# Pooled attention keys in pieces of 64, 16 and 64 turned by identity products, with a new instruction order and choice of engines

## The chip, the cores and the metric

The kernel runs on one core of one Trainium2 chip. The metric is the time of one execution on the device in microseconds (us), the median of several runs. Durations below come from one profiled execution. PE is TensorE, which multiplies; PEld is its loading of weights; DVE is VectorE, ACT ScalarE, POOL GpSimd, and SP SyncE, whose queue issues all transfers here.

## What is computed

Two parts in one kernel. First, attention over 8 batches, 8 heads, 576 positions, 64 values a head, as the sum of two attentions: one over positions pooled by four (144 of them, its output repeated four times), one in which a position sees only neighbours less than 4 away. Then an FFN on the 4608 rows that this gives, with 1024 hidden values and a SoLU with layer norm.

```python
q_d = q.reshape(B, H, Sd, factor, D).mean(axis=3)        # factor 4, Sd = 144; k_d, v_d alike
out_d = sm_attn(q_d, k_d, v_d)                           # softmax over the 144 pooled keys
out_up = np.repeat(out_d, factor, axis=2)
mask = np.abs(pos[:, None] - pos[None, :]) < factor
scores = np.where(mask, scale * np.matmul(q, k.transpose(0, 1, 3, 2)), -1e9)
out_local = softmax(scores) @ v
x = (out_up + out_local), heads side by side             # 4608 x 512
h = x @ w_in                                             # 512 x 1024
solu = h * softmax(h)
ln = (solu - mean) / np.sqrt(var + 1e-6) * g_ln
out = ln @ w_out                                         # 1024 x 512
```

The weights and g_ln are float64 as they arrive in memory. The other arrays are float32.

## The kernel before

**Attention.** A batch works on head pairs, since two heads of 64 fill 128 partitions. q and k are brought to partitions = head values (`qT`, `kT`): for the first two batches by products with the identity (`qp`, `kp`), later by the DVE's transpose of 32x32 blocks. `sums` adds each four positions (`qd`, `kd`).

`Pooled` is the pooled attention of one head pair; a batch has four. Its 144 queries are handled as 3 pieces of 48 (`QC`, `QN`). Its steps: `sd`, the scores, 6 products on 64x64 quadrants of the array; the maximum (`mxd`); the exponentials `pd` with their sums; `pd` times the reciprocal sums; `pdt`, the scores turned so that keys lie on partitions, 12 transposes of 64x72 in two halves of 72 keys; `pdT`, two copies from PSUM; `po`, 4 products of the turned scores with the pooled values `vd`, each over 72 keys; and the sum into `x`.

`Local` is the local attention of two windows of 64 positions for all heads; a batch has five. Its steps: `sc`, the scores, 16 products on quadrants; `pl`, the scores plus the mask; the maximum `mxl` and its subtraction; the exponentials; their sums `sml`, reciprocals `rsl` and the product with them; `plt`, four 128x128 transposes; `plT`, their copy; `xp`, 16 products on quadrants with the values `vw`; and the sum into `x`.

The pooled values `vd` are made of `vs`, four loads a batch of 72 pooled positions x 4 heads, each added up by two additions.

**Weights.** `Weights.piece` turns a 128x512 piece of float64 into float32 with four DVE operations and splits it into a high part and a rest (`wi_h`, `wi_l`; `wo_h`, `wo_l`), so that a product of float32 precision is three products of the faster type. There are 8 pieces of w_in and 8 of w_out; those of w_out are multiplied by g first.

**FFN.** 36 tiles of 128 rows. A tile: `xh`, `xl` are the split of `x`; `h`, 24 products of 128x512; the maximum `nmx`; the exponentials `e`; `e` times `h`; the centred values written to memory (`u`) and read back block by block (`v`); a 32x32 block transpose on DVE, the split `uh`, `ul`; `o`, 24 products with w_out; the scaled output `osb`.

**Order.** All steps of all parts are put in one list, `plan`. `ORDER` is a table of numbers that says in which order they are issued; each engine then runs its own instructions in that order and waits for what it needs. `keep_clock` issues 24 pairs of products of zeros (`warm`), which keep PE running in its idle time. Which engine runs a step is written in the step.

Of the kernel before, what the change touches and what calls it, by code (L numbers as in the profile page):

```python
# [129 lines left out]
def pooled_local_attention_then_solu_ffn(  # L130
# [31 lines left out]
    qhi = qlo[1:] + [S]  # L162

    QC = 3
    QN = SD // QC


    TILES = ((0, 0), (1, 1), (0, 1), (1, 0))
# [873 lines left out]
```

## Time and profile before

| what | value |
|---|---|
| median of 3 runs | 601.65 us (601.19 to 605.02) |
| the profiled execution, whole time | 602.74 us |
| its span in the profile | 601.0 us |
| mean granted clock of PE | 0.989 |
| busy: PE, DVE, ACT, POOL | 574.8, 396.5, 361.8, 375.6 us |
| bytes moved | 94.34 MB, 157 GB/s on average |

How to read the rows: a busy time is the sum of an engine's instructions. A product's duration reaches into the next one, since products are pipelined, so the time that a group takes is read from the starts. "A <- B" names what ended the idle time before A. A form such as 64*64 64x58 is the rows and columns of the array that a product uses, and the partitions x columns that it writes.

### The profile page before, as it was taken

How to read it: one execution, taken by the hardware profiler on the slowest of the kernel's cores; microseconds unless marked ns; L12 is line 12 of the kernel's file. 1: busy time of each engine (PE TensorE's matmuls, PEld its weight loads, DVE VectorE, ACT ScalarE, POOL GpSimd, SP SyncE). 2: the span in 40 equal slices, each digit the busy share in tenths (PEclk: the TensorE clock that was granted, in tenths of full speed). 3: DMA queues.
4: the chain of work that ended last, by engine and by line, in shares of the span. 5: the costliest groups of instructions: out<-in, count | busy, mean ns of one | idle time of the engine just before them, and what ended most of it. 6: DMA issues, size and time to landing. Idle time of an engine off the chain costs nothing.

```text
span 601.0 us, 15341 instructions
## 1 busy us (share of the span) xinstructions
PE 574.8 (96%) x5912; PEld 447.1 (74%) x5912; DVE 396.5 (66%) x692; ACT 361.8 (60%) x800; POOL 375.6 (62%) x553
## 2 busy tenths in 40 slices
PE   6889789899999999999999999999999999999996
PEld 3666557677777777787877777777777878788785
DVE  5989999869747677766856767737655533643541
ACT  3758866577745566566664854657465655553443
POOL 2576668867784778678574777656786767332221
PEclk8979999899999999999999999999999999999999
DMA  8999776687769767766878567847416623124230
GB/s 231 238 251 254 140 183 146 164 178 162 195 144 189 171 167 186 170 148 175 190 151 201 143 173 182 185 114 195 97 59 188 146 89 114 63 88 151 96 123 35
DMA packets 203913, 94.34 MB, mean 157 GB/s; under 512 B 162496, under 2 KB 192704, under 8 KB 203840
## 3 DMA queue, kind: packets, MB, share of 16 engines
q1 hardware_dynamic: 203840, 93.37, 63.3%
q8 instruction: 46, 0.75, 0.6%
q14 instruction: 27, 0.22, 0.1%
HBM read 65.54 MB, written 27.79 MB: 155 GB/s over the span
## 4 chain that ended last, share of the span: by engine, by line
PE 75%; POOL 6%; DVE 5%; ACT 4%; SPq 4%; DMA 3%; issue 3%; POOLq 0%; DVEq 0%
PE o L888 31%; PE h L770 27%; PE xp L670 3%; PE plt L660 3%; PE po L752 3%; PE sc L614 2%; DMA qm<-in_q_dram 2%; SPq L245 2%; PE pdt L731 2%; PE sd L696 2%; POOL pl L639 2%; DMA v<-u 1%; SPq L264 1%; POOL pd L720 1%; DVE w L334 1%
## 5 line engine op out<-in xcount | busy, mean ns | idle before, releaser
L888 PE MATMUL o<-wo_h,uh 128*128 128x512 f32 x288 | 117.9, 409 | 0.8 <-ACT uh L872 0.7
L770 PE MATMUL h<-wi_h,xh 128*128 128x512 f32 x288 | 116.3, 404 | 0.6 <-DVE e L785 0.6
L770 PE MATMUL h<-wi_h,xl 128*128 128x512 f32 x288 | 114.3, 397 | 1.3 <-POOL xl L922 1.3
L888 PE MATMUL o<-wo_l,uh 128*128 128x512 f32 x288 | 114.5, 398 | 0.0
L770 PE MATMUL h<-wi_l,xh 128*128 128x512 f32 x288 | 114.1, 396 | 0.0
L874 POOL TENSOR_TENSOR ul<-v,uh 128x512 fp32r<-128x512 f32 x58 | 74.4, 1288 | 19.7 <-ACT uh L872 7.7
L778 DVE TENSOR_REDUCE nmx<-h 128x1 f32<-128x1024 f32 x36 | 43.9, 1219 | 63.8 <-PE h L770 63.8
L888 PE MATMUL o<-wo_h,ul 128*128 128x512 f32 x288 | 79.1, 396 | 0.4 <-DVE ul L874 0.4
L782 ACT ACTIVATE e<-h,nmx 128x1024 f32<-128x1024 f32 x36 | 40.0, 1112 | 51.0 <-DVE nmx L778 51.0
L888 PEld LDWEIGHTS o<-wo_h,uh 128*128 128x128 f32 x288 | 54.6, 190 | 15.6 <-ACT uh L872 1.4
L770 PEld LDWEIGHTS h<-wi_h,xl 128*128 128x128 f32 x288 | 54.2, 188 | 15.2 <-POOL xl L922 2.1
L770 PEld LDWEIGHTS h<-wi_h,xh 128*128 128x128 f32 x288 | 54.2, 188 | 14.8 <-issue 1.0
L888 PEld LDWEIGHTS o<-wo_h,ul 128*128 128x128 f32 x288 | 54.2, 188 | 14.0 <-DVE ul L874 0.8
L770 PEld LDWEIGHTS h<-wi_l,xh 128*128 128x128 f32 x288 | 54.3, 189 | 12.2
L888 PEld LDWEIGHTS o<-wo_l,uh 128*128 128x128 f32 x288 | 54.5, 189 | 11.8
L922 POOL TENSOR_TENSOR xl<-x,xh 128x512 fp32r<-128x512 f32 (+1 forms) x40 | 47.1, 1183 | 18.6 <-ACT xh L919 17.4
L807 ACT ACTIVATE e<-e,nmu 128x1024 f32<-128x1024 f32 x35 | 40.1, 1146 | 28.2 <-POOL nmu L790 28.1
L785 DVE SCALAR_TENSOR_TENSOR e<-h,e 128x1024 f32<-128x1024 f32 x36 | 43.7, 1214 | 19.9 <-ACT e L782 19.9
L650 POOL TENSOR_TENSOR pl<-pl,rsl 128x512 f32<-128x512 f32 x40 | 42.1, 1055 | 20.7 <-DVE rsl L648 18.2
L866 DVE STREAM_TRANSPOSE v<-v 128x512 f32<-128x512 f32 x70 | 46.3, 688 | 12.5 <-DMA v<-u 12.5
L872 ACT ACTIVATE uh<-v 128x512 fp32r<-128x512 f32 x70 | 42.9, 623 | 14.9 <-DVE v L866 11.0
L639 POOL TENSOR_TENSOR pl<-pl,mxl 128x512 f32<-128x512 f32 x40 | 41.8, 1052 | 9.0 <-DVE mxl L637 4.6
(95 smaller groups left out, 1076.1 us busy)
## 6 DMA issues: line engine op xcount, KB each, us to landing
u<-e SPq DMA_DIRECT2D x35, 512.0 KB
v<-u SPq DMA_DIRECT2D x140, 128.0 KB
vw<-in_v_dram SPq DMA_DIRECT2D x160, 64.0 KB
vs<-in_v_dram SPq DMA_DIRECT2D x32, 288.0 KB
out_dram<-osb SPq DMA_DIRECT2D x36, 256.0 KB
qm<-in_q_dram SPq DMA_DIRECT2D x96, 72.0 KB
km<-in_k_dram SPq DMA_DIRECT2D x96, 72.0 KB
w<-in_moe_w_out_dram SPq DMA_DIRECT2D x8, 512.0 KB
```

What stands on the lines that cost most here:

```text
L639: nc.gpsimd.tensor_tensor(out=pl, in0=pl, in1=max_bc, op=ALU.subtract)
L650: nc.gpsimd.tensor_tensor(out=pl, in0=pl, in1=rs.unsqueeze(3).broadcast_to([P, NPR, 2, W]), op=ALU.mult)
L770: nc.tensor.matmul(hps[:, n, :], src[:, cc, :], wt[:, cc, n * 512:(n + 1) * 512], start=(cc == 0 and src is xh and wt is wi_h), stop=(cc = ...
L778: nc.vector.tensor_reduce(out=nmx, in_=hf, op=ALU.max, axis=AX.X, negate=True)
L782: nc.scalar.activation(e, hf, AF.Exp, bias=nmx, scale=1.0, accum_out=se)
L785: nc.vector.scalar_tensor_tensor(out=e, in0=hf, scalar=1.0, in1=e, op0=ALU.mult, op1=ALU.mult, accum_out=su)
L807: nc.scalar.activation(e, e, AF.Identity, bias=nmu, scale=1.0)
L866: nc.vector.transpose(vg, vg)
L872: nc.scalar.activation(uh, tp, AF.Copy)
L874: (nc.vector if v is None or i in LATE else nc.gpsimd).tensor_tensor(out=ul, in0=tp, in1=uh.bitcast(F32), op=ALU.subtract)
L888: nc.tensor.matmul(o, src[:, j, :], wt[:, 4 * g + j, :], start=(g == 0 and j == 0 and src is uh and wt is wo_h), stop=(g == 1 and j == 3 a ...
L922: nc.gpsimd.tensor_tensor(out=l, in0=src, in1=h.bitcast(F32), op=ALU.subtract)
```

## The change

**Pooled keys.** The 144 keys are cut into pieces of 64, 16 and 64 (`KEYS`). The turned scores of one head lie on partitions 0 to 63 and those of the other on 64 to 127. `pdt` is now 18 plain products with the identity, each on one 64x64 quadrant and 48 columns wide; `pdT` is one copy of 432 columns on 128 partitions; `po` is 6 products on quadrants. `vs` is three loads a batch (each in two transfers), and `vd` covers 128 partitions. The middle piece is loaded into one buffer, `few`, which is zeroed once. The ring of buffers `big` has 5 instead of 6.

**g.** The high part of w_out is rounded from t times g directly, and the rest is t times g minus the high part, on DVE. Before it was a product on ACT, a rounding on ACT and a subtraction on POOL.

**Engines.** A second table, `OTHER`, lists 130 steps that run on another engine than the usual one. They are 10 products `pd` x reciprocal, 11 subtractions and 14 products of `pl`, 18 `ul`, 13 `xl`, 10 sums of `vs` and 3 `wi_l` from POOL to DVE; 11 copies `plT`, 13 first sums into `x` and 3 centrings from ACT to DVE; 6 first steps of the weights' conversion (L325) from DVE to POOL; and 18 copies `pdT`, 17 of which go from DVE to ACT and one from ACT to DVE.

**Order.** `ORDER` is new throughout.

```diff
-        return load.tile([P, 1024], F32, tag="big", name=name, bufs=6)
+        return load.tile([P, 1024], F32, tag="big", name=name, bufs=5)
...
+    KEYS = ((0, 64), (64, SD - 128), (SD - 64, 64))
+    ORDER_C = (0, 2, 1)
...
+    few = cpool.tile([P, 1024], F32, name="few")
+    nc.gpsimd.memset(few, 0.0)
+    def engine(usual, instead):
+        return instead if now[0] in other else usual
...
+    def load_vs(b, c):
+        (p0, n), name = KEYS[c], f"vs_{b}_{c}"
+        vs = (big(name) if n == 64 else few).rearrange("p (r x) -> p r x", r=NPR)
+        for par in range(2):
+            nc.sync.dma_start(
+                vs[rows(par)][0:n],
+                v[b, par::2, FAC * p0:FAC * (p0 + n), :].rearrange("h (p t) d -> p h (t d)", t=FAC),
+            )
...
-            nc.vector.tensor_scalar(
+            engine(nc.vector, nc.gpsimd).tensor_scalar(
                 out=t, in0=t, scalar1=F64_LO, scalar2=F64_HI, op0=ALU.max, op1=ALU.min
             )
...
-                nc.scalar.activation(t, t, AF.Copy, scale=self.g[:, fc:fc + 1])
+                    nc.scalar.activation(hi, t, AF.Copy, scale=g)
+                    yield
+                    nc.vector.scalar_tensor_tensor(
+                        out=lo, in0=t, scalar=g, in1=hi.bitcast(F32), op0=ALU.mult, op1=ALU.subtract
+                    )
...
-                nc.gpsimd.tensor_tensor(out=pl, in0=pl, in1=max_bc, op=ALU.subtract)
+                engine(nc.gpsimd, nc.vector).tensor_tensor(
+                    out=pl, in0=pl, in1=max_bc, op=ALU.subtract
+                )
...
-            for kc in range(2):
-                for j in range(QC):
-                    for x in range(2):
-                        c = (2 * j + x) % QC
-                        nc.tensor.transpose(
-                            pt[:, x, kc, j, :], pd[rows(x), (0, 2, 1)[c], kc * 72:(kc + 1) * 72],
-                            ident[rows(x), rows(x)],
+            for kc, (k0, _) in enumerate(KEYS):
+                for c in ORDER_C:
+                    for par in (0, 1):
+                        src = rows(par ^ (c == 2))
+                        nc.tensor.matmul(
+                            pt[rows(par), c, kc, :],
+                            pd[src][0:QN, c, k0:k0 + 64],
+                            ident[src][0:QN, src][:, 0:QN], start=True, stop=True,
                         )
...
-            nc.scalar.activation(pdT[:, :, :, 0, :], pt[:, 0], AF.Copy)
-            yield
-            if b < 2:
-                nc.scalar.activation(pdT[:, :, :, 1, :], pt[:, 1], AF.Copy)
-            else:
-                nc.vector.tensor_copy(out=pdT[:, :, :, 1, :], in_=pt[:, 1])
+            copy(
+                engine(nc.scalar, nc.vector) if b < 2 else engine(nc.vector, nc.scalar),
+                pdT.rearrange("p k j n -> p j k n"), pt,
+            )
...
-            for kc in range(2):
+            for kc, (_, n) in enumerate(KEYS):
                 for par in range(2):
...
+                    at = rows(par)
+                    nc.tensor.matmul(
+                        po[at, :], bt.vd[at][0:n, kc, pr, :], pdT[at][0:n, kc, :],
+                        start=kc == 0, stop=kc == len(KEYS) - 1,
+                    )
...
+        now[0] = int(n)
+        fn, args = plan[now[0]]
         fn(*args)
```

What the new order does on an engine is seen at three places. The first is PE in the last batch, near the end of its pooled attention. Before (the number behind a name is the tile's; `x12` counts equal products that follow each other):

```order
L670 MATMUL xp_4_7336<-plT_4_7327,vw_4_6685 64x56 x16
L731 MATMUL pdt_2_7356<-ident,pd_2_7132 72x64 x12
L752 MATMUL po_0_7375<-pdT_0_7161,vd_6837 64x144 x4
L731 MATMUL pdt_1_7380<-ident,pd_1_6892 72x64 x12
L696 MATMUL sd_3_7401<-kd_6051,qd_flat 64x144 x6
L752 MATMUL po_2_7411<-pdT_2_7369,vd_6837 64x144 x4
L770 MATMUL h_7416<-wi_h,xh_7126 128x512
```

The same place on PE with the change:

```order
L729 MATMUL xp_4_7572<-plT_4_7570,vw_4_6613 64x56 x16
L729 MATMUL xp_3_7596<-plT_3_7323,vw_3_7591 64x58 x16
L809 MATMUL po_0_7613<-pdT_0_7416,vd_7387 64x144 x6
L791 MATMUL pdt_3_7621<-ident,pd_3_7543 64x48 x18
L791 MATMUL pdt_1_7643<-ident,pd_1_7181 64x48 x18
L809 MATMUL po_2_7663<-pdT_2_7452,vd_7387 64x144 x6
L827 MATMUL h_7551<-wi_h,xh_7325 128x512
```

Before, groups of three shapes follow each other, and each changes the array's shape; now six groups of one shape stand together.

The second place is DVE at the program's start, with the first two pieces of w_in (`w_2`, `w_0`). Before:

```order
L325 TENSOR_SCALAR w_2_131<-w_2_131 128x512
L329 TENSOR_SCALAR w_2_131<-w_2_131 128x512
L325 TENSOR_SCALAR w_0_145<-w_0_145 128x512
L334 SCALAR_TENSOR_TENSOR w_2_131<-w_2_126,w_2_131 128x512
L338 SCALAR_TENSOR_TENSOR w_2_131<-w_2_126,w_2_131 128x512
L329 TENSOR_SCALAR w_0_145<-w_0_145 128x512
```

DVE at the start with the change:

```order
L359 TENSOR_SCALAR w_0_138<-w_0_138 128x512
L363 TENSOR_SCALAR w_0_138<-w_0_138 128x512
L368 SCALAR_TENSOR_TENSOR w_0_138<-stage,w_0_138 128x512
L372 SCALAR_TENSOR_TENSOR w_0_138<-stage,w_0_138 128x512
L359 TENSOR_SCALAR w_2_150<-w_2_150 128x512
L363 TENSOR_SCALAR w_2_150<-w_2_150 128x512
L405 TENSOR_TENSOR wi_l<-w_0_138,wi_h 128x4x4x32
```

The pieces come in the other order, and the rest of piece 0 (`wi_l`) is now taken on DVE between them instead of on POOL.

The third place is DVE in the fifth batch, around the sums of the local windows. Before:

```order
L778 TENSOR_REDUCE nmx_4189<-h_4164 128x1
L644 TENSOR_REDUCE sml_3_4196<-pl_108 128x8
L648 RECIPROCAL rsl_3_4198<-sml_3_4196 128x8
L785 SCALAR_TENSOR_TENSOR e_4218,su_4221<-h_4164,e_4218 128x1024
L743 COPY pdT_0_4213<-pdt_0_4200 72x6x48
```

The same window on DVE with the change:

```order
L703 TENSOR_REDUCE sml_3_4280<-pl_108 128x8
L707 RECIPROCAL rsl_3_4282<-sml_3_4280 128x8
L835 TENSOR_REDUCE nmx_4298<-h_4267 128x1
L777 RECIPROCAL rsd_0_4316<-smd_0_4230 128x3
L779 TENSOR_TENSOR pd_0_4229<-pd_0_4229,rsd_0_4316 128x432
L709 TENSOR_TENSOR pl_108<-pl_108,rsl_3_4282 128x4x128
L412 TENSOR_REDUCE kd_4193<-kT_4097 128x144
L842 SCALAR_TENSOR_TENSOR e_4319,su_4329<-h_4267,e_4319 128x1024
```

Two products that stood on POOL (`pd` and `pl` times their reciprocals) now stand in DVE's queue between the maximum of `h` and the product of `e` and `h`.

More of the change, by code (lines that the diff above doesn't have):

```diff
@@ L219, in pooled_local_attention_then_solu_ffn, with copy @@
         nc.vector.memset(pl, 1e-9)
+    few = cpool.tile([P, 1024], F32, name="few")
+    nc.gpsimd.memset(few, 0.0)
     qd_flat = cpool.tile([P, NPR * SD + 64 - QN], F32, name="qd_flat")
     nc.vector.memset(qd_flat[:, NPR * SD:], 0.0)
+    other = {int(n) for n in OTHER.split()}
+    now = [None]
+    def engine(usual, instead):
+        return instead if now[0] in other else usual
+    def copy(eng, out, in_):
+        if eng is nc.scalar:
+            nc.scalar.activation(out, in_, AF.Copy)
+        else:
+            eng.tensor_copy(out=out, in_=in_)
     def two_banks(pool, tag, name):
@@ L233, in small_bank @@
     def small_bank(b, n):
-        return (ps_o, "o") if b < 2 and n % 2 and not W_PSUM and not WARM else (ps_t, "t")
+        return (ps_o, "o") if b < 2 and n % 2 and not WARM else (ps_t, "t")
     def load_q_k(t, b, pr):
@@ L389, in __getattr__ @@
             elif what == "vd":
[L390 removed]
+                self.vd = att.tile([P, len(KEYS), NPR, D], F32, tag="vd", name=f"vd_{self.b}")
             else:
@@ L483, in pair_steps @@
                 yield
-                nc.scalar.activation(
+                copy(
+                    engine(nc.scalar, nc.vector),
                     dst.rearrange("x (p a t) -> x p a t", a=2, t=HT),
-                    tp[:, :, 0:n].rearrange("x a (t p) -> x p a t", t=HT), AF.Copy
+                    tp[:, :, 0:n].rearrange("x a (t p) -> x p a t", t=HT),
                 )
                 yield
-            sums(self.qd[pr], self.qT[:, pr])
+            if self.b >= SUM_PE:
+                sums(self.qd[pr], self.qT[:, pr])
+                yield
+                sums(self.kd[:, pr], self.kT[:, pr])
+                yield
+                return
+            sp = ps_t.tile([P, 2, SD], F32, tag="t", name=f"qs_{self.b}_{pr}")
+            for n, src in enumerate((self.qT, self.kT)):
+                by_four = src[:, pr].rearrange("x (s f) -> x s f", f=FAC)
+                for f in range(FAC):
+                    nc.tensor.matmul(
+                        sp[:, n], ident, by_four[:, :, f], start=f == 0, stop=f == FAC - 1
+                    )
             yield
-            sums(self.kd[:, pr], self.kT[:, pr])
+            for n, dst in enumerate((self.qd[pr], self.kd[:, pr])):
+                copy(engine(nc.scalar, nc.vector), dst, sp[:, n])
             yield
@@ L495, in accumulate @@
         if first:
-            nc.scalar.activation(x, part, AF.Copy)
+            copy(engine(nc.scalar, nc.vector), x, part)
         else:
@@ L662, in by_tensor @@
             plT = wk.tile([P, NPR, 2, W], F32, tag="plT", name=f"plT_{b}_{u}")
-            nc.scalar.activation(plT, pt, AF.Copy)
+            copy(engine(nc.scalar, nc.vector), plT, pt)
             yield
@@ L806, in ffn_in @@
         else:
-            nc.scalar.activation(e, e, AF.Identity, bias=nmu, scale=1.0)
+            if engine(nc.scalar, nc.vector) is nc.scalar:
+                nc.scalar.activation(e, e, AF.Identity, bias=nmu, scale=1.0)
+            else:
+                nc.vector.tensor_scalar(
+                    out=e, in0=e, scalar1=1.0, scalar2=nmu, op0=ALU.mult, op1=ALU.add
+                )
         s = small.tile([P, 1], F32, tag="s", name=f"s_{i}", bufs=6)
@@ L975, in values @@
     def values(bt):
-        for m in range(4):
-            hs = slice(m // 2 * 4, m // 2 * 4 + 4)
-            step(bt.pooled_vload, m % 2, hs)
-            step(bt.pooled_vsum, m % 2, hs)
+        for c in range(len(KEYS)):
+            step(bt.pooled_vload, c)
+            step(bt.pooled_vsum, c)
     def attention(bt):
+        late = bt.b == 0
+        local = [Local(bt, u, not late) for u in range(5)]
+        pooled = [Pooled(bt, pr, late) for pr in range(NPR)]
         values(bt)
-        local = [Local(bt, u, bt.b > 0) for u in range(5)]
-        pooled = [Pooled(bt, pr, bt.b == 0) for pr in range(NPR)]
-        for it in pooled + local if bt.b == 0 else local + pooled:
+        for it in pooled + local if late else local + pooled:
             if isinstance(it, Local):
                 step(bt.load_v, it.u)
-            row(it.steps(), 10 if isinstance(it, Pooled) or bt.b < MASKED else 11)
+            row(it.steps(), 9 if isinstance(it, Pooled) else 11 - (bt.b < MASKED))
     tiles = 0
```

82 lines of the change are left out of this document (41 added, 41 removed), and 203 rows, old and new, of tables (ORDER, OTHER).

## The prediction

> **What bounds the kernel now.** I read the page's busy shares and its chain first, then the windows by stage, then the waits of TensorE, and last the chain in order of time.
>
> ```profile
> PE 574.8 (96%) x5912; PEld 447.1 (74%) x5912; DVE 396.5 (66%) x692; ACT 361.8 (60%) x800; POOL 375.6 (62%) x553
> PE 75%; POOL 6%; DVE 5%; ACT 4%; SPq 4%; DMA 3%; issue 3%; POOLq 0%; DVEq 0%
> ```
>
> 96% busy is an average over stages. In the windows (columns: length, then busy time and count of PE, weight loads, DVE, ACT, POOL, then clock, DMA share, GB/s) the stages differ:
>
> ```profile
> 15.00:60.00 45.00, 39.03 (x761) 29.90 (x756) 41.05 (x72) 33.28 (x94) 28.73 (x27) 0.92 1.02 248
> 60.00:120.00 60.00, 51.18 (x748) 39.26 (x741) 57.11 (x94) 41.23 (x82) 45.37 (x50) 0.97 0.72 159
> 120.00:360.00 240.00, 239.54 (x2434) 187.84 (x2435) 165.76 (x297) 151.18 (x351) 169.88 (x249) 1.00 0.73 172
> 360.00:560.00 200.00, 198.99 (x1788) 156.58 (x1784) 109.94 (x192) 114.46 (x241) 121.81 (x192) 1.00 0.47 126
> ```
>
> From 15 to 120 us DVE is busy 41.05 + 57.11 = 98.2 of 105 us (93%) and PE has gaps. From 120 to 560 us PE is busy 438.5 of 440 us, and what it still waits for there is this (waits of PE from 120 to 590 us: total, times, longest):
>
> ```profile
> PE sc L614 <- issue: 0.9, 1, 0.9
> PE o L888 <- DVE ul L874: 0.4, 1, 0.4
> PE pdt L731 <- ACT pd L711: 0.3, 1, 0.3
> ```
>
> So the kernel has a start set by DVE and, behind it, a PE stage with 1.6 us of waits. There a microsecond of PE work is a microsecond of time, and relieving ACT or POOL brings nothing.
>
> **PE, group by group.** The chain in order of time gives each group from the end of the one before it to its own end (start, us, what, records):
>
> ```profile
> 361.11 1.09 PE sc L614 x64
> 362.20 0.59 PE plt L660 x4
> 362.79 0.62 PE xp L670 x32
> 363.40 3.01 PE o L888 x12
> 366.41 0.62 PE xp L670 x32
> 367.03 0.47 PE sc L614 x32
> 367.50 0.64 PE po L752 x8
> 368.14 0.80 PE pdt L731 x24
> 368.94 5.81 PE o L888 x24
> 374.75 0.64 PE po L752 x8
> 375.39 0.46 PE pdt L731 x12
> ```
>
> ```profile
> 248.48 1.13 PE sd L696 x24
> ```
>
> And by form (columns: products, rows*columns of the array, count, busy, mean ns):
>
> ```profile
> L614 PE MATMUL sc<-kT,qT 64*64 64x64 f32 x1280 | 27.5, 225 | 2.3 <-DVE pl L632 1.4 <-issue 0.9
> L670 PE MATMUL xp<-plT,vw 64*64 64x58 f32 x1024 | 21.8, 226 | 0.3 <-ACT pd L711 0.3
> L731 PE MATMUL pdt<-ident,pd 64*72 64x64 f32 x384 | 16.5, 221 | 2.1 <-POOL wi_l L362 1.3 <-ACT kT L484 0.5 <-ACT pd L711 0.3
> ```
>
> Three readings. First, a group costs less behind one of its own shape: sc takes 0.47 behind xp (both 64*64) where xp takes 0.62 behind o; the second sc of the 1.09 takes 0.47 as well, the second sd 1.13 - 0.64 = 0.49 (a lone one is like po's 0.64), the second pdt 0.80 - 0.46 = 0.34. Coming from another shape thus costs 0.15 (pdt 0.12). Second, an f32 product of this kind is two records (16 products of sc are 32 records), a transpose is one (12 are 12). Third, records on different quadrants run side by side: 32 records on four quadrants are 8 rounds, 0.47 / 8 = 0.059 a round, and with 64 columns (sc) no longer than with 58 (xp); sd's 12 records put four on its fullest quadrant, 0.49 / 4 = 0.122 a round at 144 columns.
>
> **The change on PE.** The 12 transposes of a pair (0.34 without the entry) become 18 products of 48 columns, so 36 records; two of the three query pieces use the same two quadrants, so 12 rounds. Nothing in the trace is 48 columns wide. If a round shrinks with its columns from sd's, it is 0.122 x 48/144 = 0.041 and the group 0.49; if it stays where sc and xp are, 0.059 and 0.70. I take 0.70, the nearest row, as 58 and 64 columns already cost the same, and keep 0.49 as the other end. The Trainium skill (TensorEngine Tiling (Array Packing), Performance Considerations, Instruction Overhead) says that a product has about 60 cycles of overhead, so that one column takes as long as 60. By it the piece is 0.70, without it 0.49 and the sum 5 us less; the equal rows of sc and xp agree with it, and no run here shows fewer columns.
>
> po's 4 products become 6. Three go to each of two quadrants, two records each: 6 rounds of 0.122 = 0.73, against 0.64 - 0.15 = 0.49. The middle piece has only 16 keys, but its 144 columns stream all the same.
>
> From the fifth FFN tile on the order holds 24 of each in both kernels, all in the full PE stage. That adds 24 x 0.36 = 8.6 and 24 x 0.24 = 5.8 us. Against it, all small products are now 64*64 and the new order sets them beside each other: counted in PE's order over this stretch, entries from another shape fall from 75 at 0.15 plus 22 at 0.12 (13.9 us) to 50 at 0.15 (7.5 us), which is 6.4 less. **PE sum: +8.0 us** (+2.9 with the 0.49). The eight pooled pairs ahead of that stretch fall where PE has gaps (51.18 busy of 60), and cost nothing as long as DVE sets the pace.
>
> **The change on DVE.** The moved work comes from POOL, mostly:
>
> ```profile
> L325 DVE TENSOR_SCALAR w<-w 128x512 f32<-128x512 f32 x16 | 12.9, 814 | 5.6 <-ACT w L323 5.6
> L334 DVE SCALAR_TENSOR_TENSOR w<-w,w 128x512 int32<-128x512 int32 x12 | 8.0, 682 | 0.1
> L632 DVE TENSOR_TENSOR pl<-sc,mask 128x512 f32<-128x512 f32 x40 | 26.7, 675 | 12.8 <-PE sc L614 12.7
> L703 DVE TENSOR_REDUCE mxd<-sd 128x3 f32<-128x432 f32 x32 | 18.8, 590 | 6.8 <-PE sd L696 6.7
> L743 DVE COPY pdT<-pdt 72x288 f32<-72x288 f32 x24 | 10.6, 444 | 14.5 <-ACT pdT L738 14.5
> L362 POOL TENSOR_TENSOR wi_l<-w,wi_h 128x512 fp32r<-128x512 f32 x8 | 11.0, 1375 | 24.1 <-ACT wi_h L360 24.1
> L434 POOL TENSOR_TENSOR vs<-vs 72x512 f32<-72x512 f32 x32 | 41.4, 1293 | 0.6
> ```
>
> **Start.** Ahead of the fifth tile's first product, DVE gets 8 wo_l and 3 wi_l subtractions (11 at 0.68 = 7.5), and one pd, two pl, one ul, one xl and one pdT (about 0.65 each, 3.9); it loses 6 of the L325 rows (6 x 0.814 = 4.9) and four reductions that now stand later (about 0.65 each, 2.6). That is +3.9, on an engine that was 93% busy, so **+4 us**. Ends: -4 (DVE's 6.8 us of gaps up to 120 us are partly filled) and +8.
>
> **Middle, 120 to 360 us.** Up to the twenty-first tile, about that stretch, DVE further gets 7 pd (0.6, as mxd over the same 432 columns), 13 pl (0.675), 14 ul and xl (0.68), 6 first sums of v (0.68), 5 second ones (half as wide, 0.37), 13 copies of plT and x (512 and 464 columns, 0.65), and loses eight of 13 pdT copies, the rest being longer (-2.8): +34 us, 200 of 240, 83%. PE waits on a queue that full now and then; no row prices it. Its ends are 0, since DVE keeps 40 us to spare, and +17 (rival 1); I take **+3**, near the 1.6 that PE waits now. Behind a delayed subtraction on DVE stand the transposes of v and with them the o products, so a late one reaches PE.
>
> ACT loses a copy a pair and the w_out scaling, POOL about a third of its work; from 120 us on both are idle enough (151 and 170 of 240) that this brings nothing. Bytes moved stay the same, and the 48 idle-time products stay 48. The ring of big buffers has five instead of six, and the middle keys share one buffer, so some loads of v start later. I cost that at nothing, since they are issued well ahead and the DMA engines are 73% and 47% busy from 120 us on; without that cover a late load holds its sums and one po by about a flight:
>
> ```profile
> 89.77 3.15 DMA vw<-in_v_dram
> ```
>
> **Sum.** The profiled execution took 602.74 us; 602.7 + 8.0 + 4 + 3 = 617.7. The median of the runs is 1.1 lower, so **616.6 us**. With the start from 0 to 8 and the waits from 0 to 6 it is 610 to 624.
>
> **Rivals.**
>
> 1. DVE becomes the bound of the middle stage. Speaking for it, the same instruction with and without POOL at work:
>
> ```profile
> 10.65 0.69 DVE L334 SCALAR_TENSOR_TENSOR w<-stage,w 128x512 int32<-128x512 int32 x1
> 11.09 1.37 POOL L362 TENSOR_TENSOR wi_l<-w,wi_h 128x512 fp32r<-128x512 f32 x1 [8.57 <-ACT wi_h L360]
> 11.37 1.64 DVE L338 SCALAR_TENSOR_TENSOR w<-stage,w 128x512 int32<-128x512 int32 x1
> ```
>
> The second DVE row starts inside POOL's and takes 1.64 where its like takes 0.69: 0.95 more. 45 of the operations added between 120 and 360 us read two SBUF tiles as these do. If each met POOL, DVE would need 200 + 43 = 243 of 240 us; at the start's 93% filled that is 261, or 21 more. About half of the PE sum, 4, lies in this stretch and would be covered, so the wait is 17 in place of 3: 630.6. It decides once DVE passes 93% of 244 us, 227: 0.6 us more for each of the 45. Against it: POOL itself gets emptier, and most such rows in the trace are short (mean 0.682). The Trainium skill (GPSIMD Engine Reference, Specifications) has POOL share its SBUF interfaces with VectorE, with contention for DVE instructions in a 2-port mode or with two SBUF inputs; that speaks against the move of this work, and the 1.64 agrees.
>
> 2. Narrow rounds do scale (0.49) and the start comes out even: 602.7 + 2.9 - 1.1 = 604.5, no difference. For it: no row excludes 0.041.
>
> 3. Faster: POOL, not DVE, sets the start. The chain runs on POOL alone from 25.65 to 41.0 us, 13 pieces:
>
> ```profile
> 25.65 1.28 POOL wi_l L362
> ...
> 40.00 1.00 POOL pl L650
> ```
>
> Ahead of the fifth tile POOL loses 8 wo_l and 3 wi_l (1.3 each), two pairs of vs and vd (1.3 and about 0.7) and five others (about 1.2), 24 us, and gets 6 of the L325 operations (unknown there; 1.3 like its others): -17. If all of it came through: 602.7 - 17 + 2.9 - 1.1 = 587.5. It decides from 14 us gained before 120 us with a PE sum of 8. Against it: POOL was busy 74 of the 105 us, DVE 98.
>
> 4. The new products do not run side by side: 36 x 0.059 = 2.1 a pair, 24 x 1.4 = 34 us more, 650. sc and xp, placed alike, speak against it.
>
> **How the numbers follow.** Forecast 0.50, rival 1 0.14, rival 2 0.22, rival 3 0.12, rival 4 0.02. About 1% is what a measurement of this kernel can tell from none, so faster 0.12, same 0.22, slower 0.66. The range reaches down to rival 2 with its own spread and up over rival 1: 596 to 632, leaving out rivals 3 and 4 and a part of rival 1.
>
> **What would show it.** pdt at 0.70 (0.49: rival 2) and po at 0.73 in a run of 64*64 groups; sc and xp at 0.47 more often than before; the first h product, in the trace of before at
>
> ```profile
> 62.91 0.50 PE L770 MATMUL h<-wi_h,xh 128*128 128x512 f32 x1
> ```
>
> about 4 us later; DVE near 83% from 120 to 360 us; PE's waits there of a few us. I am wrong if PE reaches its full stage earlier than 120 us, or if DVE shows rows of 1.6 us by the dozen.

## The result, and the profile after

| | before | after |
|---|---|---|
| median | 602.33 us (601.19 to 605.02, 4 runs) | 630.25 us (629.37 to 634.11, 4 runs) |
| ratio after / before | | 1.0469, 95% interval 1.0412 to 1.0527 |
| span of the profiled execution | 601.0 us | 627.5 us |
| fifth FFN tile's first product | 128.29 us | 142.22 us |
| from there to the end of the span | 472.7 us | 485.3 us |

The change made the kernel 4.7% slower. It lies in the range given, near its top, and 13.7 us above the forecast. Of the 26.5 us that the span grew, 13.9 are there by the fifth tile and 12.6 come behind it. The page of after, busy shares and chain by engine:

```profile
PE 597.4 (95%) x6808; PEld 460.3 (73%) x6808; DVE 480.0 (76%) x795; ACT 339.9 (54%) x749; POOL 287.7 (46%) x446
PE 76%; DVE 14%; DMA 3%; issue 3%; ACT 2%; POOL 1%; SPq 0%; POOLq 0%; DVEq 0%; ACTq 0%
```

In the chain DVE has gone from 5% to 14% and POOL from 6% to 1%. The windows of after, the same stages as before:

```profile
15.00:60.00 45.00, 38.37 (x716) 27.17 (x716) 42.58 (x67) 29.03 (x79) 29.11 (x23) 0.86 0.93 223
60.00:120.00 60.00, 50.32 (x752) 38.44 (x749) 59.09 (x89) 33.60 (x75) 40.46 (x39) 0.94 0.68 152
120.00:360.00 240.00, 235.81 (x2809) 183.13 (x2809) 196.83 (x334) 134.67 (x299) 113.94 (x185) 1.00 0.73 169
360.00:560.00 200.00, 200.00 (x2181) 156.74 (x2180) 143.11 (x244) 108.50 (x246) 84.81 (x143) 1.00 0.45 121
```

From 60 to 120 us DVE is busy 59.09 of 60 (57.11 before). From 120 to 360 it is at 196.83 of 240, 82%, and PE hardly notices. These are all of PE's waits in after from the fifth tile to the end (total, times, longest):

```profile
PE o L951 <- ACT uh L934: 1.2, 2, 0.7
PE h L827 <- ACT xh L982: 0.4, 1, 0.4
PE h L827 <- DVE e L842: 0.2, 1, 0.2
```

The first product of the fifth tile, in before's timeline and in after's:

```profile
128.29 0.40 PE L770 MATMUL h<-wi_h,xh 128*128 128x512 f32 x1
```

```profile
142.22 0.50 PE L827 MATMUL h<-wi_h,xh 128*128 128x512 f32 x1 [0.35 <-ACT xh L982]
```

So there are two places: a start in which DVE has more to do, and a full PE stage that has become longer in itself.

**The start.** The time from the span's start to the fifth tile, in one window each; first the trace of before, then that of after:

```profile
0.00:128.30 128.30, 108.46 (x1665) 80.33 (x1666) 113.11 (x194) 84.74 (x194) 82.14 (x95) 0.95 0.85 199
```

```profile
0.00:142.20 142.20, 117.48 (x1908) 83.89 (x1908) 129.16 (x202) 78.51 (x179) 79.59 (x86) 0.93 0.78 183
```

DVE has 8 instructions more (202 for 194) and is busy 16.1 us more (129.16 for 113.11); it idles 13.0 us in place of 15.2, and 16.1 less 2.2 are the 13.9. Which instructions, in the groups of that window of after:

```profile
L368 DVE SCALAR_TENSOR_TENSOR w<-w,w 128x512 int32<-128x512 int32 x12 | 12.7, 1062 | 0.1
L372 DVE SCALAR_TENSOR_TENSOR w<-w,w 128x512 int32<-128x512 int32 x12 | 12.1, 1012 | 0.1
L363 DVE TENSOR_SCALAR w<-w 128x512 int32<-128x512 int32 x16 | 10.7, 667 | 0.7 <-POOL w L359 0.4
...
L397 DVE SCALAR_TENSOR_TENSOR wo_l<-w,g_sb,wo_h 128x512 fp32r<-128x512 f32 x8 | 7.5, 950 | 0.0
...
L359 DVE TENSOR_SCALAR w<-w 128x512 f32<-128x512 f32 x10 | 6.4, 644 | 5.6 <-ACT w L357 5.6
```

The first two are the bit operations of the weights' conversion, which the change does not touch: before, they are L334 and L338, 24 of 0.68. They now take 24.8 us in place of 16.0. A stretch of after's timeline shows what stretches them (start, duration):

```profile
42.64 1.06 POOL L480 TENSOR_TENSOR vd<-few 128x256 f32<-128x256 f32 x1
43.04 1.21 DVE L368 SCALAR_TENSOR_TENSOR w<-w,w 128x512 int32<-128x512 int32 x1
...
43.66 1.72 POOL L477 TENSOR_TENSOR vs<-vs 128x512 f32<-128x512 f32 x1
44.17 0.68 DVE L689 TENSOR_TENSOR pl<-sc,mask 128x512 f32<-128x512 f32 x1
44.77 1.16 DVE L372 SCALAR_TENSOR_TENSOR w<-w,w 128x512 int32<-128x512 int32 x1
```

L368 starts while POOL runs and ends 0.55 after POOL's instruction has (43.70); L372 starts inside the next one (to 45.38) and ends 0.55 behind it as well. Between them L689, which reads one of its inputs from PSUM, takes its usual 0.68 beside the same POOL instruction. Counted over all bit operations, the eight on staged pieces among them, 2 of 32 start while POOL runs in before, 15 of 32 in after. Of these 15, 14 end 0.55 behind POOL's instruction; the other 17 take 0.69 in the mean, none over 0.75. I call this holding.

**The full stage.** The chain of after, with the second of two neighbouring pdt in the 1.53:

```profile
399.13 0.83 PE pdt L791 x36
399.96 1.04 PE po L809 x12
...
526.38 1.53 PE pdt L791 x72
```

pdt behind its own shape is 1.53 - 0.83 = 0.70, as forecast. po behind pdt is 1.04, where 0.73 was forecast. Its groups by form suggest why:

```profile
L809 PE MATMUL po<-pdT,vd 64*64 64x144 f32 x256 | 28.8, 301 | 0.0
...
L809 PE MATMUL po<-pdT,vd 16*64 16x144 f32 x128 | 14.8, 306 | 0.0
```

The products with 16 keys use another form of the array, between two of the first form. From the fifth tile on, with the times from the first record of a group to the first of the next added up by name: pdt 10.8 to 18.0 (+7.2), po 15.4 to 22.9 (+7.5), everything else -2.1, together the 12.6.

### The profile page after: what moved, and what is told of

Its sections match the earlier page's. It is cut to its first block, busy times and chain, and to the rows that moved or that the text cites. A ratio compares the mean times of both kernels' runs of the same rounds, so it can differ in the third digit from the quotient of the medians.

```text
span 627.5 us, 17058 instructions
## 1 busy us (share of the span) xinstructions
PE 597.4 (95%) x6808; PEld 460.3 (73%) x6808; DVE 480.0 (76%) x795; ACT 339.9 (54%) x749; POOL 287.7 (46%) x446
## 4 chain that ended last, share of the span: by engine, by line
PE 76%; DVE 14%; DMA 3%; issue 3%; ACT 2%; POOL 1%; SPq 0%; POOLq 0%; DVEq 0%; ACTq 0%
PE o L951 29%; PE h L827 27%; PE po L809 4%; PE pdt L791 3%; PE sc L671 3%; PE xp L729 3%; DVE w L368 3%; PE plt L719 3%; PE sd L755 2%; DVE w L372 2%; DMA stage<-in_moe_w_in_dram 1%; DMA u<-e 1%; DVE w L363 1%; DVE wo_l L397 1%; DVE w L359 1%
## 5 line engine op out<-in xcount | busy, mean ns | idle before, releaser
L951 PE MATMUL o<-wo_l,uh 128*128 128x512 f32 x288 | 113.7, 395 | 0.7 <-DVE wo_l L397 0.7
L827 PE MATMUL h<-wi_l,xh 128*128 128x512 f32 x288 | 113.7, 395 | 0.0
L827 PE MATMUL h<-wi_h,xl 128*128 128x512 f32 x288 | 113.7, 395 | 0.0
L937 POOL TENSOR_TENSOR ul<-v,uh 128x512 fp32r<-128x512 f32 x40 | 53.1, 1328 | 53.9 <-ACT uh L934 40.9
L827 PEld LDWEIGHTS h<-wi_l,xh 128*128 128x128 f32 x288 | 54.1, 188 | 11.8
L865 ACT ACTIVATE e<-e,nmu 128x1024 f32<-128x1024 f32 x32 | 36.7, 1146 | 24.2 <-POOL nmu L847 24.2
L985 POOL TENSOR_TENSOR xl<-x,xh 128x512 fp32r<-128x512 f32 (+1 forms) x26 | 31.7, 1220 | 28.4 <-ACT xh L982 28.2
L709 POOL TENSOR_TENSOR pl<-pl,rsl 128x512 f32<-128x512 f32 x26 | 29.0, 1120 | 30.4 <-DVE rsl L707 27.7
L696 POOL TENSOR_TENSOR pl<-pl,mxl 128x512 f32<-128x512 f32 x29 | 31.0, 1070 | 20.1 <-DVE mxl L694 19.6
```

Of the source, the lines that this page charges most:

```text
L696: engine(nc.gpsimd, nc.vector).tensor_tensor(out=pl, in0=pl, in1=max_bc, op=ALU.subtract)
L709: engine(nc.gpsimd, nc.vector).tensor_tensor(out=pl, in0=pl, in1=rs.unsqueeze(3).broadcast_to([P, NPR, 2, W]), op=ALU.mult)
L827: nc.tensor.matmul(hps[:, n, :], src[:, cc, :], wt[:, cc, n * 512:(n + 1) * 512], start=(cc == 0 and src is xh and wt is wi_h), stop=(cc = ...
L865: nc.scalar.activation(e, e, AF.Identity, bias=nmu, scale=1.0)
L937: (usual if v is None else engine(usual, nc.vector)).tensor_tensor(out=ul, in0=tp, in1=uh.bitcast(F32), op=ALU.subtract)
L951: nc.tensor.matmul(o, src[:, j, :], wt[:, 4 * g + j, :], start=(g == 0 and j == 0 and src is uh and wt is wo_h), stop=(g == 1 and j == 3 a ...
```

## Experiments

All times below, medians and the two parts of each profiled execution:

| kernel | median, us | ratio to before (95%) | fifth tile at | from there on | DVE busy until the fifth tile |
|---|---|---|---|---|---|
| before | 602.33 | | 128.3 | 472.7 | 113.1 |
| after | 630.25 | 1.047 (1.041 to 1.053) | 142.2 | 485.3 | 129.2 |
| po on 64 rows | 623.55 | 1.034 (1.030 to 1.039) | 141.9 | 479.2 | 128.5 |
| old engines in the start | 649.14 | 1.076 (1.072 to 1.080) | 158.9 | 487.0 | 114.1 |
| short POOL work | 617.38 | 1.024 (1.019 to 1.028) | 131.6 | 485.9 | 113.3 |
| bit operations together | 631.15 | 1.050 (1.043 to 1.057) | 142.6 | 485.3 | 127.9 |
| clips on DVE, po on 64 rows | 625.44 | 1.035 (1.030 to 1.040) | 144.8 | 479.0 | 128.8 |
| new pieces, old order | 621.80 | 1.029 (1.024 to 1.034) | 137.8 | 483.5 | 113.7 |
| the same with g late | 624.84 | 1.033 (1.028 to 1.037) | 140.4 | 482.5 | 121.4 |
| old pieces, new order | 625.00 | 1.035 (1.030 to 1.041) | 146.4 | 477.0 | 129.1 |
| before, pdt twice | 603.95 | 1.002 (0.999 to 1.005) | 129.6 | 472.3 | 113.6 |
| before, five big buffers | 607.29 | 1.007 (1.004 to 1.010) | 127.5 | 476.0 | 114.7 |
| before, short POOL work | 594.82 | 0.987 (0.985 to 0.990) | 120.9 | 471.5 | 105.0 |

**po's middle product on 64 rows.**

```diff
-            for kc, (_, n) in enumerate(KEYS):
+            for kc, n in enumerate((64, 64, 64)):
                 for par in range(2):
```

> The change's kernel with one edit: po's middle product takes all 64 rows of the array instead of 16 (the rows beyond 16 are zero in vd, so the sum is the same). Shape theory: a 16-row product between 64-row ones empties the array twice, and that is why po took 0.93 to 1.04 us where 0.73 was forecast. Then po falls to about 0.73 and 24 to 32 pairs give back 0.3 each: 7 to 9 us, so 621 to 623 us. Rival, the six rounds are simply that long (a longer weight load, the accumulation in one bank): po stays at 0.93 or more and the time at 629 to 631 us.

The chain of this kernel at the same po, and its one group:

```profile
395.81 0.83 PE pdt L791 x36
396.64 0.75 PE po L809 x12
```

```profile
L809 PE MATMUL po<-pdT,vd 64*64 64x144 f32 x384 | 29.7, 286 | 0.0
```

0.75 for 1.04 with the same number of products: 0.29 a pair, 24 x 0.29 = 7.0, and the stretch behind the fifth tile got 6.1 shorter. The shape theory holds: the rows left out of the middle product cost more than they save. The Trainium skill (TensorEngine Tiling (Array Packing), Key Properties) has a change of the tiling mode drain TensorE; the trace agrees, with 0.29 us for the two changes of a pair.

**The prices by themselves.** Behind the last step of after, on DVE eight of each kind alone and then beside POOL; on TensorE groups like po and pdt.

```diff
+    for fn in (bits_sbuf, bits_psum, clip):
+        fn()
+    nc.vector.tensor_copy(out=x1, in_=y0)
+    for _ in range(45):
+        nc.gpsimd.tensor_tensor(out=x0, in0=x0, in1=x1, op=ALU.mult)
+    for fn in (bits_sbuf, bits_psum, clip):
+        fn()
...
+    po_like((64, 64, 64)); po_like((64, 16, 64)); po_like((16, 16, 16))
+    pdt_like(16); pdt_like(48); pdt_like(72); pdt_like(96)
```

> The change's kernel with two measurements behind its last step (its own time means nothing). First, on DVE eight each of the bit operation on w with both inputs in SBUF, the same with one input in PSUM, and a clip (one input), 128x512, at first alone and then beside 45 POOL products of two SBUF tiles. Holding theory: alone 0.68, about 0.7 and 0.4 us; beside POOL the first stretches to about 1.5 us, the one with a PSUM input stays at 0.7, the clip (one input) goes to at most 0.8. If all DVE work slows beside POOL alike, the PSUM one stretches as well. Second, on TensorE six each of po-like groups with 64, 64, 64 rows, with 64, 16, 64 and with 16, 16, 16, and 18-product groups like pdt with 16, 48, 72 and 96 columns. Shape theory: 0.73, 1.0 and 0.7 us a group. Rounds that do not shrink: 16 and 48 columns both about 0.70 us a group, 72 and 96 columns about 0.7 to 1.0; rounds in proportion to columns: 0.25 us at 16.

DVE's timeline, eight in a row: the bit operation with both inputs in SBUF (L1082), with one in PSUM (L1087), the clip (L1092). First alone:

```profile
619.77 5.76 DVE L1082 SCALAR_TENSOR_TENSOR pl<-pl,pl 128x512 int32<-128x512 int32 x8
625.57 5.74 DVE L1087 SCALAR_TENSOR_TENSOR pl<-pl,bank 128x512 int32<-128x512 int32 x8
631.34 3.66 DVE L1092 TENSOR_SCALAR pl<-pl 128x512 f32<-128x512 f32 x8
```

Then beside POOL (the first of the L1082 still ran before POOL had begun):

```profile
635.49 12.43 DVE L1082 SCALAR_TENSOR_TENSOR pl<-pl,pl 128x512 int32<-128x512 int32 x8
647.96 5.74 DVE L1087 SCALAR_TENSOR_TENSOR pl<-pl,bank 128x512 int32<-128x512 int32 x8
653.73 10.91 DVE L1092 TENSOR_SCALAR pl<-pl 128x512 f32<-128x512 f32 x8
```

Two SBUF inputs: 0.69 alone, 1.64 each beside POOL. One input in PSUM: 0.69 both times. So DVE is not slower as such beside POOL; what is held is the instruction with two SBUF inputs, and the clip with one, 0.43 to 1.38, which I had put at 0.8 at most. The Trainium skill (SBUF — State Buffer, Who interferes with whom) has the two engines share a pair of ports as an exclusive lock, for two SBUF inputs and for DVE's 2-port modes, into which a one-input operation can get; the three pairs of rows agree.

On TensorE a po-like group comes every 0.735 us with 64, 64, 64 rows, every 1.028 with 64, 16, 64, and every 0.735 with 16, 16, 16 (read from the starts of its records). It is the change of shape that costs, not the small product. For the pdt-like groups, these are windows of the products with 16 and then with 48 columns, six groups each, in which these products alone are counted:

```profile
638.80:646.40 7.60, 7.60 (x219) 7.60 (x220) 0.00 (x0) 0.00 (x0) 0.50 0.02 4
646.40:654.09 7.69, 7.69 (x222) 7.69 (x224) 0.00 (x0) 0.00 (x0) 0.50 0.01 2
```

Both take 1.27 to 1.28 us a group, at a granted clock of 0.50, so a product of 16 columns is as long as one of 48. Rival 2's shrinking rounds do not exist here, and the Trainium skill's rule that the forecast weighed (TensorEngine Tiling (Array Packing), Performance Considerations, Instruction Overhead) agrees. A group with 72 columns took 1.44 at that clock; if its time is in proportion to its columns, 1.28 us are 64 of them, so by this estimate columns count from about 64 on.

**Short POOL work in the start.**

```diff
+    def eighth(eng, ap):
+        cut = eng is nc.gpsimd and now[0] in start
+        return ap[..., 0:ap.shape[-1] // 8] if cut else ap
...
-                    out=pl, in0=pl, in1=max_bc, op=ALU.subtract
+                    out=eighth(eng, pl), in0=eighth(eng, pl), in1=eighth(eng, max_bc), op=ALU.subtract
```

> The change's kernel, in which POOL's subtractions and scalings of pl, its scalings of pd and its first sums of v ahead of the fifth FFN tile cover an eighth of each row's elements, so that they are short; the rest of these is left out. DVE's instructions are all the same. Holding theory: a DVE instruction that reads two SBUF tiles and starts while POOL runs is held until POOL is through (1.2 to 1.8 us in place of 0.68), 14 us of it up to the fifth tile. Then the bit operations on w fall from about 1.07 to 0.7 us, the fifth tile comes at 130 to 134 us, and the time is 618 to 622 us. Amount theory: DVE's work at its undisturbed length sets the start; rows that were long stay long, fifth tile at 140 or later, time 627 to 631 us.

This kernel and the control below leave out the other seven eighths of POOL's rows, so what they compute is not the reference. DVE's groups up to the fifth tile, the two bit operations and wo_l:

```profile
L374 DVE SCALAR_TENSOR_TENSOR w<-w,w 128x512 int32<-128x512 int32 x12 | 9.3, 785 | 0.1
...
L378 DVE SCALAR_TENSOR_TENSOR w<-w,w 128x512 int32<-128x512 int32 x12 | 8.7, 722 | 0.1
...
L403 DVE SCALAR_TENSOR_TENSOR wo_l<-w,g_sb,wo_h 128x512 fp32r<-128x512 f32 x8 | 5.7, 727 | 0.0
```

They fall to nearly their lengths alone, DVE has 15.9 us less up to the fifth tile (113.3 for 129.2), and the tile comes 10.6 earlier. Taken by itself that agrees with holding as the cause of the late start. But short POOL work also shortens chains through POOL, and before has held instructions too. Hence a control.

**The same cut in the kernel before.** The edit is the same, in the functions of before.

> A control: the kernel before with the same of POOL's work cut to an eighth of each row ahead of the fifth tile as in the change's kernel with short POOL work (subtractions and scalings of pl, scalings of pd, first sums of v; the rest of them is left out). There the cut freed 16 us of DVE and brought the fifth tile 10.6 us forward. If holding by POOL is what the change added, the cut has less to give here: DVE's bit operations are not held before (24 at 0.68), only the clips and shifts (32 at 0.70 where 0.43 is their length alone, 8.6 us) and the first bit operations of the staged pieces (1.9 us). About 10 us of DVE at two thirds is 7 us at most; I expect 3 to 7: fifth tile at 121 to 125, 595 to 599 us. If short POOL work simply shortens the start's chains in any kernel, 10 us or more as there: fifth tile at 118 or earlier, 592 us or less. If nothing: 128 and 602 us, and the whole of the 10.6 us there is the change's.

Here the cut frees 8.1 us of DVE (113.1 to 105.0) and brings the tile 7.4 forward: what DVE got back are the clips and shifts (32 at 0.70, now 0.44 in the mean); the bit operations had nothing to give. So of the 10.6 us in after, 7.4 are to be had in the kernel before as well. What the change added, by this measure, is 15.9 - 8.1 = 7.8 us of DVE, but only 10.6 - 7.4 = 3.2 us of the start, because other waits then show (DVE idles 18.3 us up to the tile, 13.0 in after).

**The bit operations one behind another.**

```diff
 order of the steps of each weight piece
-    abs, clip, shift ... first bit operation ... second bit operation
+    abs, clip ... shift, first bit operation, second bit operation
```

> The change's kernel with another order of a few of DVE's steps: for each piece of a weight the shift, and the two bit operations on w stand one right behind another, as most did before the change, instead of among other DVE work. Holding theory: only the first of two neighbours is then held by POOL, the second goes through at 0.69 us, so the second's mean falls from 1.04 to about 0.7 and the start gains about 4 us: 625 to 627 us. Amount theory: the same number of instructions at the same length, 629 to 631 us.

Nothing: 631.15, fifth tile at 142.6. The second operations of the eleven pairs behind 15 us fell from a mean of 1.04 only to 0.94. My step, that only the first of two neighbours waits, is wrong: of the six pairs behind 15 us whose first operation waits, the second waits as well in four, since POOL's next instruction gets in between. The measurement of the prices shows the two engines strictly by turns, seven DVE operations of 1.64 between POOL's of 1.60.

**Old engines in the start.**

```diff
-    G_LATE = True
+    G_LATE = False
 and in OTHER, 20 steps up to about the fifth tile are left out
```

> The change's kernel with the old engines up to about the fifth FFN tile: the subtractions of wi_l and wo_l back on POOL (g as ACT's scaling of w again), and the clips of w, one pd, two pl, two ul, three xl and one sum of v where they were before. The new order, the pooled pieces and all later choices stay. Engine theory: the start is late (fifth tile's first product at 142.2 us, 128.3 before) through what was put on DVE, whose moved rows took about 14 us there; taking them away brings the fifth tile to 130 to 134 us and the time to 618 to 622 us. Amount theory (only the undisturbed 3.9 us that I had counted): about 626 us. Order theory: the new order alone makes the start late, and the time stays at 629 us or more.

The engine theory fell: 649.14, fifth tile at 158.9, although DVE's work went back to 114.1 us. Neither DVE nor POOL is full then; they wait in their order. POOL's two longest waits from 15 to 160 us:

```profile
POOL wo_l L404 <- ACT wo_h L402: 29.1, 6, 7.1
POOL wi_l L404 <- ACT wi_h L402: 22.1, 5, 6.9
```

and DVE waits 11.8 us for po, and PE 5.0 us with po for POOL's vd. As I read it, in this order a subtraction on POOL stands ahead of work that others wait for. The moves to DVE are thus not the fault by themselves; order and engines belong together.

**The clips back on DVE** (on top of po on 64 rows).

```diff
 in OTHER, the six first steps of the weights' conversion are left out
```

> The change's kernel with po's middle product on 64 rows (623.6 us measured) and the six clips of w that the change gave to POOL (1.95 us each there) back on DVE. Chain theory: the bit operations on w wait for the clip on POOL, and POOL's 12 us hold DVE; DVE gets 6 x 0.4 to 0.75, and the start gains 3 to 6 us: 618 to 621 us. Amount theory: DVE has 3 to 4.5 us more to do: 626 to 628 us.

625.44 against 623.55 of its base, fifth tile at 144.8 for 141.9. No gain from a shorter chain, though the 12 us less on POOL left DVE at 128.8 us (128.5): the clips' own time used up what less holding gave (10 of the 32 bit operations start while POOL runs, 14 in its base). The two intervals overlap, so only "not faster" is shown.

**The new pieces in the old order, without and with g late.**

```diff
-14 3 175 159 160 23 19 8 161 176 ...        (the new table)
+the steps in before's order; pdT's copy at the place of the first of two;
+the three sums of v at the places of before's first two; OTHER empty; po on 64 rows
-    G_LATE = True
+    G_LATE = False                           (True in the second of the two)
```

> Only the pooled pieces of the change, in the old order on the old engines: pieces of 64, 16 and 64 keys turned by products, one copy of them (in the place of the first of the two), sums of v in three pieces, all three in the place of the first two of before, po's middle product on 64 rows, g applied as before. Theory: the PE terms stand as forecast (24 x 0.36 for pdt and 24 x 0.24 for po) without the new order's fewer changes of shape, 14 us less up to 4 for pdt's own entries, and the start is that of before (fifth tile at 126 to 131 us): 612 to 617 us. Rival, the pieces themselves disturb the start (sums of v on 128 partitions, DVE's copies): fifth tile at 135 or later and 620 us or more.

> As the old order with only the pooled pieces, and in it also g at w_out's rounding: the eight wo_l subtractions on DVE as one operation with g, ACT's scalings gone. Holding and amount theory: 8 DVE operations of 0.68 to 0.95 us more on an engine that sets the start, 5 to 8 us later than the old order alone. Rival, POOL sets the start (it loses 8 x 1.3): 5 us earlier or more. Neither: within 2 us.

Both start late, at 137.8 and 140.4, with DVE's work at 113.7 as before: the rival's result, but through my own placing. The chain of the first one begins with two loads of v:

```profile
7.73 11.30 DMA vs<-in_v_dram
...
19.05 11.23 DMA vs<-in_v_dram
...
30.41 1.27 POOL vs L471
```

All of a batch's sums stand where before's first two stood, so po and the subtractions of pl wait for a load that lands at 30.28 us. Its start therefore says nothing of the change's. Its second part takes 483.5 from the fifth tile on, 4.3 more than with the new order and the same po (479.2). Most of that is waits: PE waits 5.6 us there, and 2.3 in the other. The three longest:

```profile
PE sc L665 <- issue: 2.2, 1, 2.2
PE h L821 <- POOL xl L979: 1.1, 1, 1.1
PE po L803 <- DVE x L549: 1.0, 1, 1.0
```

Changes of shape are not what the new order saves. Counted in PE's order over this stretch, the small groups that come from another shape are 97 in before, 52 here, and 50 with the new order: it is the pieces that make them fewer. With g late DVE has 7.7 us more up to the fifth tile, and that comes 2.6 later; in the medians the two are not told apart.

**The old pieces in the new order on the new engines.**

```diff
-            for kc, (k0, _) in enumerate(KEYS):
...
+                        nc.tensor.transpose(
+                            pt[:, x, kc, j, :], pd[rows(x), (0, 2, 1)[c], kc * 72:(kc + 1) * 72],
+                            ident[rows(x), rows(x)],
+                        )
```

> The other half of the change: its order, its engines and g at w_out's rounding, but the pooled keys in the two pieces of 72 with the transposes and two products of before, sums of v and loads on 72 partitions and six big buffers (the two copies of pdT stand together). Theory: DVE is held by POOL in the start as in the change (13 us), the pieces' part of the start is gone, fifth tile at 134 to 139 us; behind it pdt gives back 24 x 0.36 and po 24 x 0.54, and 15 to 25 more entries between shapes take 3 to 4 of that, so 466 to 470 us from there and 602 to 609 us in all. Rival, the order itself makes the start late whatever the pieces: fifth tile at 141 or later, 610 us or more.

The rival again: 146.4, later than with the new pieces, with the same 129.1 us on DVE. So order, engines and g make the start late without the pieces, and with six big buffers. From the fifth tile on it takes 477.0, 4.3 more than before, and that is no price of the order: PE waits 4.6 us (2.3 in before), and from 247.0 to 250.4 us its granted clock is 0.51, in no other of these profiles. For the same reason the 2.2 us up to the new pieces on 64 rows (479.2) are not the pieces' price. Added up by name, pdt and po take about 7 us more with them (34.5 for 27.4).

**Before with pdt twice, and with five buffers.**

```diff
-            for kc in range(2):
+            for kc in (0, 1, 0, 1) if b < 2 else (0, 1):
```

> The kernel before with the transposes of the first eight pooled pairs issued twice (same data, same place), 0.34 us more of TensorE work a pair, about the length that the products take. Cover theory (mine in the forecast): TensorE has gaps ahead of the fifth tile, so 602 us as before, within 1.5. Chain theory: the start runs through TensorE too (DVE waits for pdt, po and sd in order), so 2.7 us more of work show nearly in full, 604.5 us or more, fifth tile at 130 or later.

```diff
-        return load.tile([P, 1024], F32, tag="big", name=name, bufs=6)
+        return load.tile([P, 1024], F32, tag="big", name=name, bufs=5)
```

> The kernel before with five instead of six buffers in the ring for weights and sums of v. Cover theory (mine in the forecast): loads are issued early enough, 602 us within 1.5, fifth tile at 128. Load theory: a ring one shorter holds loads back in the start, where the DMA engines are full, and that is the delay of the old order with the new pieces (fifth tile at 137.8): 606 us or more.

Longer products ahead of the fifth tile are covered: 1.002 with an interval about 1, the tile 1.3 later for 2.7 us of work. The fifth buffer's absence is not: 1.007 (1.004 to 1.010), about 4 us, and in the profile it shows behind the fifth tile (476.0 for 472.7), 2.1 of it in small waits of PE (4.4 for 2.3), not in the start where I looked for it.

## Why the forecast was off

The direction and the two places were right, and the time within the range; the size was half of what came. That the range holds it is partly luck: the spread of the sum itself ended at 624, and the range went further for rival 1, which is not what happened. (That spread took the start from 0, although its lower end had been put at -4.)

- **PE, pdt.** 0.70 by the nearest row, measured 0.70; columns under 64 save nothing. Right.
- **PE, po.** 0.73 forecast, 1.04 measured. The step that failed is "its 144 columns stream all the same": they do, but I let the 16-row product count as 64*64. It changes the array's shape twice a pair, and I had the price of such changes in hand: where 50 entries from another shape were counted, PE's order holds 50 + 48. 24 x 0.29 = 7 us. With the product on 64 rows the stretch takes 479.2, +6.5, where PE sum and waits were put at 8 + 3. For the same reason the six groups that the text ahead of the forecast calls one shape are not: each po holds a 16-row product. And the fewer entries, 6.4 us, were credited to the new order as well; the pieces alone, with po on 64 rows, bring them from 97 to 52.
- **PE waits in the middle.** 3 more forecast; from the fifth tile on PE waits 1.8 us in all, 2.3 in before, so nothing was added. DVE's share was right, 82% for 83%. Rival 1 did not come in the middle stage: behind the fifth tile only two of DVE's moved operations take over 1.4 us (1.78 and 1.50). Its time, 630.6, is almost the one measured, and that is chance. The sign that I had named for it, long rows by the dozen, came in the start: 15 bit operations that wait, up to 1.80 us.
- **The start.** +4 forecast, with ends of -4 and +8; +13.9 measured (first product of h at 68.77 us, +5.9). I had quoted the held row, 1.64 for 0.69, and used it only for rival 1 between 120 and 360 us. For the start I priced the moved work at its length alone and, above all, left the operations that were already there at theirs. Of DVE's 16.1 us more, 8.8 are the 24 bit operations; the eight wo_l took 7.5 in place of 5.4, and one pd and two pl 4.6 in place of 1.9. What such instructions meet changes with the order as well as with the engines: of the 32 bit operations 9 start while POOL runs with the old engines in the start, and 4 with the new pieces in the old order on the old engines (15 in after, 2 in before).
- **Five buffers at nothing.** In the kernel before they cost 0.4 to 1.0%. In the change's kernel this was not tried by itself, nor was the one buffer that the middle keys share.
- **The eight early pairs at nothing.** About right: in before, 2.7 us more of such work brought the tile 1.3 later, and in the change's kernel 8 x 0.29 = 2.3 us less of it (po on 64 rows) brought it 0.3 earlier.
- **Rival 3.** No gain from a relieved POOL: up to the fifth tile it is busy 79.59 us in after, 82.14 in before, and the start is longer all the same. POOL was hardly relieved, 17 us less being forecast: a clip, for one, costs it 1.95, where I had put 1.3. Where it was relieved, in before with short POOL work (82.1 to 54.0 us), the tile came 7.4 earlier, but with 8.1 us less on DVE and DVE's idle time as it was (15.2 and 15.9): DVE still set the start.

Shown is that the bit operations are held by POOL, by how much, and that DVE has 16.1 us more in the start. How the 13.9 us divide between holding, order and engines is not settled: with the old engines the fifth tile came 16.7 later than in after, with the old pieces 4.2 later, and the cut of POOL's work, set against its control, explains 3.2. The parts do not add up, since each kernel's order was left as it was and waits took the place of work. The kernel has a switch, `W_PSUM`, that puts one input of the bit operations in PSUM; with it on, holding could be taken from them without touching POOL's work. That was not run.

No version tried that computes the reference is faster than before.

## What to carry to other kernels

Read a small product's array shape with the sizes of its operands: padding 16 keys with zeros to the neighbours' 64 rows was worth 6.7 us here. When work moves between DVE and POOL, or only its order, price every two-input and every fast one-input DVE instruction in the stage that DVE bounds at its held length too, also those that the change leaves alone; one PSUM input takes an instruction out of this. And an order table and its engine choices are one thing: putting back a part of the engines cost 19 us.

## What the runs showed of the hardware

A clip of 128x512 takes 0.43 us alone and 1.38 beside POOL's steady work, a threefold price, more than the 0.69 to 1.64 of the two-input operation. Under that load the engines take strict turns, so grouping DVE's held instructions does not help. And TensorE's granted clock stood at 0.50 from 638 to 658 us although it had no idle time: it fell about 4 us after the 16-row products had begun (633.8), stayed low with products of 48 rows by 16 and 48 columns, and rose about 4 us after those with 72 columns had begun (654.1). In this kernel's own stage of wide products it stays at 1.00.
